# Keys of four chunks loaded instead of transposed, and weights queued in whole pieces, in a retention, mixture and MLP kernel

## The chip, the cores and the metric

The kernel runs on one core of one Trainium2 chip. The metric is the device time of one execution in microseconds (us); lower is better. The kernel before takes 447.51 us (median of 3 runs, 447.18 to 447.83). Beside the runs one execution was profiled, and all rows below come from it.

## The reference

Three parts follow each other. First a linear attention with decay ("retention"), over 4 batches, 8 heads, 768 tokens and 64 features per head; then a soft mixture of 8 experts with 4 slots each; then a two-layer MLP with a sigmoid gate. All is computed in single precision.

```python
def _attn_ref(q, k, v):                       # q, k, v: [4, 8, 768, 64]
    gamma = 1.0 - 2.0 ** (-5.0 - np.arange(H))
    for t in range(S):
        state = gamma * state + einsum('bhd,bhe->bhde', k[:, :, t], v[:, :, t])
        y[:, :, t] = scale * einsum('bhd,bhde->bhe', q[:, :, t], state)

def _moe_ref(x, phi, w1, w2):                 # x: [3072, 512], w1: [8, 512, 1024], w2: [8, 1024, 512]
    logits = x @ phi
    d = softmax(logits over tokens);  slot_input = d.T @ x
    for e in range(8): slot_out[e] = maximum(slot_input[e] @ w1[e], 0) @ w2[e]
    c = softmax(logits over slots);   return c @ slot_out

def _moe2_ref(x, w_in, w_out):                # w_in: [512, 2048], w_out: [2048, 512]
    h = x @ w_in
    return (h / (1 + exp(-1.702 * h))) @ w_out
```

## The kernel before, in words

The kernel has three stages in time. The **retention stage** goes through 24 chunks of 128 tokens (4 batches of 6). The **expert stage** runs the 8 experts on 32 slot inputs; its weights `w1` and `w2` come in 32 pieces of 1 MB. The **MLP stage** takes the rest of the time, on TensorE.

*A chunk.* For chunk i `stage_a` forms the score products of keys and queries (line 211, sixteen matmuls), and VectorE masks them (L215). `stage_v` scales the values on GpSimd (L229). One step later `stage_b` computes the output from the running state (L256) and from the scores (L260), and then adds this chunk's keys times values to the state (L268), except in the last chunk of a batch. `stage_c` transposes the output (L281). Every fourth chunk adds logits (L313) and an outer product (L371).

*Keys, twice.* The score products want the keys with features on the partitions, as they are stored in `ktv`. The state update wants them with tokens on the partitions. That second form comes in one of two ways, which the table `KTP` chooses for each chunk. For a chunk in `KTP`, TensorE transposes the keys it already has (L222, four matmuls into a tile `kp`), and ScalarE copies them out (L223). For any other chunk `load_b` loads them from `kt` in memory (L200, 256 KB).

*Loads.* All loads of this stage are issued by SyncE, in the order of the program, and wait there for their buffer. For chunk i + 2 these are `load_a`: keys and values together (`ktv`, L186, 512 KB in rows of 4 KB) and then the queries (`qt`, L188, 256 KB in rows of 2 KB). There are three buffers of each, so a load waits for chunk i - 1 to be done with its buffer: for the queries that is the state product of that chunk (L256).

*Weights among the chunks.* Seventeen of the 32 weight pieces are loaded in this stage, into 14 buffers of a pool `wp` and 3 of a pool `wq`. `load_half` does it in halves: L129 allocates a piece and loads its first half (512 KB, rows of 4 KB), L124 the second. In every step i > 0 the main loop issues halves, ahead of the step's other loads, until a line through 34 halves at i = 23 is reached. Five more pieces go into the space that the retention tiles leave at the end, and the last ten into buffers of `wp` that the first expert matmuls free; these come through `load_piece` (L137), one transfer of 1 MB with rows of 8 KB, but for the last piece.

TensorE runs its instructions in program order. The order within a step is: scores of i, transposed keys of i if i is in `KTP`, output and state of i - 1, transposed output of i - 2.

Of the kernel before, what the change touches and what calls it, by code (L numbers as in the profile page):

```python
# [24 lines left out]
NI = B * NC  # L25
# [8 lines left out]
NW = 14  # L34
NQ = 3
# [3 lines left out]
FULL = (2, 6, 7)  # L39
Q = 256  # L40
NWU = 3
I0 = 1
SKEW = 128
KTP = (0, 1, 2, 3, 8, 13, 16, 20)
BUD = 2.3
C1, C2 = 0.34, 0.6
WL = (3, 2)
# [3 lines left out]
def retention_soft_moe_mlp(  # L51
# [17 lines left out]
    def pool(stack, name, bufs, **kw):  # L69
        e = ctx.enter_context(ExitStack())  # L70
        kw.setdefault("reuse_waits", "tile")
        if "space" not in kw:
            kw["side"] = "left" if stack is left else "right"
        t = e.enter_context(tc.tile_pool(name=name, bufs=bufs, **kw))
        return t, e
# [4 lines left out]
    wp, _ = pool(left, "wp", NW)  # L80
    sm, sm_e = pool(right, "sm", 2)
    xx, xx_e = pool(right, "xx", 5)
    wq, wq_e = pool(left, "wq", NQ)
# [3 lines left out]
    def wt(tag, shape, name):  # L87
        return fresh.pop(tag, None) or wk.tile(shape, F32, tag=tag, name=name)
# [32 lines left out]
    def load_half(pool):  # L121
        if half:
            t, src = half.pop()
            nc.sync.dma_start(out=t[:, 2:4], in_=src[:, 2:4])  # L124
            return
        kind, e, k = pieces.pop()
        t = pool.tile([P, 4, 512], F32, tag="w", name=f"{kind}_{e}_{k}")
        src = (w1 if kind == "w1" else w2)[e, k, :, 0:2048].rearrange("p (j f) -> p j f", j=4)
        nc.sync.dma_start(out=t[:, 0:2], in_=src[:, 0:2])  # L129
        W[kind, e, k] = t  # L130
        half.append((t, src))

    def load_piece(pool, tag="w"):
        kind, e, k = pieces.pop()
        t = pool.tile([P, 4, 512], F32, tag=tag, name=f"{kind}_{e}_{k}")
        src = (w1 if kind == "w1" else w2)[e, k, :, 0:2048].rearrange("p (j f) -> p j f", j=4)
        nc.sync.dma_start(out=t, in_=src)  # L137
        W[kind, e, k] = t
# [36 lines left out]
    def load_a(i):  # L175
        if i < NI:
            src = ktv[i, :, 0:1024].rearrange("p (a t) -> p a t", a=2)
            if i == 2:
                early.append(wp.tile([P, 4, 512], F32, tag="w", name="early"))
                ktv_t[i] = early[0][:, 0:2]  # L180
            else:
                ktv_t[i] = wt(f"ktv{i % 3}", [P, 2, 512], f"ktv{i}")
            if i < 2:
                nc.sync.dma_start(out=ktv_t[i][:, 0], in_=src[:, 0])
            else:
                nc.sync.dma_start(out=ktv_t[i], in_=src)  # L186
            qt_t[i] = wt(f"qt{(i + 1) % 3}", [P, NP, P], f"qt{i}")
            nc.sync.dma_start(out=qt_t[i], in_=qt[i, :, 0:512].rearrange("p (a t) -> p a t", a=NP))  # L188
# [4 lines left out]
    def load_b(i):  # L193
        if i < NI and i % NC < NC - 1:
            if i == 3:
                t = early[0][:, i].rearrange("p (h d) -> p h d", h=H)
            else:
                t = wt(f"kt{(i - i // NC) % 3}", [P, H, D], f"kt{i}")
            if i not in KTP:
                nc.sync.dma_start(out=t, in_=kt[i, :, 0:512].rearrange("p (h d) -> p h d", h=H))  # L200
            kt_t[i] = t
# [3 lines left out]
    def stage_a(i):  # L205
        q_, kv = qt_t[i], ktv_t[i]
        kT = kv[:, 0].rearrange("p (a t) -> p a t", a=NP)
        sc = [ps.tile([P, NP, P], F32, tag=f"sc{hh}", name=f"sc{hh}_{i}") for hh in range(2)]
        for a in range(NP):
            for hh in range(2):  # L210
                mm(sc[hh][:, a, :], lhsT=kT[hh * D:(hh + 1) * D, a, :], rhs=q_[hh * D:(hh + 1) * D, a, :],  # L211
                   start=True, stop=True)
        pt = [wt(f"pt{hh}{i % 2}", [P, NP, P], f"pt{hh}_{i}") for hh in range(2)]
        for hh in range(2):
            nc.vector.tensor_tensor(  # L215
                out=pt[hh], in0=sc[hh], in1=mask[:, None, :].to_broadcast([P, NP, P]), op=ALU.mult
            )
        p_t[i] = pt
        if i in KTP and i % NC < NC - 1:
            kp = ps.tile([P, NP, P], F32, tag="m", name=f"kp{i}", bufs=3)  # L220
            for a in range(NP):
                nc.tensor.transpose(kp[:, a, :], kT[:, a, :], ident)  # L222
            nc.scalar.copy(out=kt_t[i].rearrange("p h d -> p (h d)"), in_=kp.rearrange("p a t -> p (a t)"))  # L223

    def stage_v(i):
        c = i % NC
        v_ = ktv_t.pop(i)[:, 1].rearrange("p (h d) -> p h d", h=H)
        vt = wt(f"vt{i % 2}", [P, H, D], f"vt{i}")
        nc.gpsimd.tensor_tensor(  # L229
            out=vt, in0=v_, in1=vs[:, c, :, None].to_broadcast([P, H, D]), op=ALU.mult  # L230
        )
        vt_t[i] = vt
        if c == 0:
            tb_t[i] = tab
        else:
            tb_t[i] = wt("tb", [P, NP, P], f"tb{i}")
            nc.gpsimd.tensor_tensor(
                out=tb_t[i], in0=tab, in1=gsc[:, :, c, None].to_broadcast([P, NP, P]), op=ALU.mult
            )
# [3 lines left out]
    def stage_b(i):  # L243
        c = i % NC
        q_, vt, pt = qt_t.pop(i), vt_t.pop(i), p_t.pop(i)
        y = ps.tile([P, 2, 512], F32, tag="y", name=f"y{i}")

        def out_(a, hh):
            o = hh ^ (a & 1)
            return y[o * D:(o + 1) * D, a % 2, P * (a // 2):P * (a // 2) + P]  # L250

        if c > 0:
            for a in range(NP):
                for hh in range(2):
                    r = slice(hh * D, (hh + 1) * D)
                    mm(out_(a, hh), lhsT=s_sb[r, a, :], rhs=q_[r, a, :], start=(a < 2), stop=False,  # L256
                       skip_group_check=True)
        for a in range(NP):
            for hh in range(2):
                mm(out_(a, hh ^ (a & 1)), lhsT=vt[:, 2 * a + (hh ^ (a & 1)), :], rhs=pt[hh ^ (a & 1)][:, a, :],  # L260
                   start=(c == 0 and a < 2), stop=True, skip_group_check=True)
        if c < NC - 1:
            if c == 0:
                st_p[0] = ps.tile([P, NP, D], F32, tag="st", name=f"st{i}")
            st, k_ = st_p[0], kt_t.pop(i)
            for a in range(NP):
                for hh in range(2):
                    mm(st[hh * D:(hh + 1) * D, a, :], lhsT=k_[:, 2 * a + hh, :], rhs=vt[:, 2 * a + hh, :],  # L268
                       start=(c == 0 and a == 0), stop=True, skip_group_check=True)
            nc.scalar.copy(out=s_sb, in_=st)  # L270
        xT = xx.tile([P, NP, P], F32, tag="xT", name=f"xT{i}")
        nc.vector.tensor_tensor(
            out=xT.rearrange("p (s k) t -> p k s t", k=2), in0=y[:, :, 0:2 * P].rearrange("p k (s t) -> p k s t", s=2),
            in1=tb_t.pop(i).rearrange("p (s k) t -> p k s t", k=2), op=ALU.mult,
        )
        xT_t[i] = xT
# [578 lines left out]
    with tc.manual_schedule():  # L855
# [18 lines left out]
        loaded = 0  # L874
        ex_t = {}
        for i in range(NI + 2):
            if i == 2:
                stage_b(1)
            if i < NI:
                stage_a(i)  # L880
                stage_v(i)
                while i > 0 and loaded < min(2 * (NW + NQ), 2 + i * 2 * (NW + NQ) // (NI - I0)):
                    load_half(wp if loaded < 2 * NW else wq)
                    loaded += 1
                load_b(i + 1)
                load_a(i + 2)
            if i >= 8 and i % 4 == 0 and i < NI:
                ex_t[i // 4 - 2] = row_softmax(i // 4 - 2)
            if i >= 9 and i % 4 == 1 and i < NI:
                row_norm(i // 4 - 2, ex_t.pop(i // 4 - 2))  # L890
            if 1 <= i <= NI and i != 2:
                stage_b(i - 1)
            if i >= 2:
                n = i - 1
                g = n // 4 - 1
                if i < NI + 1:
                    stage_c(i - 2)
                else:
                    lp = stage_g1(g, True)
                    stage_c(i - 2, True)  # L900
                    softmax_stats(g, lp)
                    combine1()
                    last_z = stage_g2(g)
                    stage_c2(i - 2)
                if n % 4 == 0 and i <= NI:
                    stage_g1(g)
                if n % 4 == 1 and n > 4:
                    stage_g2(g)
                if n % 4 == 2 and 4 < n < 22:
                    stage_g3(g)  # L910
# [340 lines left out]
```

## Time and profile before

| | |
|---|---|
| runs | 447.51 us median (447.18 to 447.83) |
| profiled execution | 446.99 us |
| its span, first to last instruction | 445.2 us |
| TensorE busy | 433.4 us, 97% |
| VectorE busy | 333.6 us, 75% |
| ScalarE busy | 205.2 us, 46% |
| GpSimd busy | 47.9 us, 11% |
| moved by DMA | 92.38 MB, mean 208 GB/s |

The profile names engines PE (TensorE), DVE (VectorE), ACT (ScalarE), POOL (GpSimd) and SP (SyncE). A busy share over the whole span mixes the stages, so the page also cuts the span into 40 slices. "Share" of the DMA engines is the time that their packets took, as a part of the time of 16 engines; packets overlap a little, so it can stand above 1.

### The profile page before, as it was taken

The numbers are of one execution on the slowest core, as the hardware profiler recorded it, in microseconds if no ns is written. First come the engines' busy times: TensorE is split into PE (matmuls) and PEld (weight loads), VectorE is DVE, ScalarE is ACT, GpSimd is POOL, SyncE is SP. The second block draws the span as 40 slices with busy tenths as digits, with TensorE's granted clock in tenths as the row PEclk, the third lists the DMA queues.
The fourth block names the chain that finished last, engine by engine and source line by source line (L and its number), as shares of the span: only waits on it lengthen the run. The fifth ranks groups of instructions, "written<-read, shape, count | busy, mean of one in ns | idle before, by whom it ended". The sixth has DMA issues, their size and how long they took to land.

```text
span 445.2 us, 9917 instructions
## 1 busy us (share of the span) xinstructions
PE 433.4 (97%) x4105; PEld 359.8 (81%) x4105; DVE 333.6 (75%) x600; ACT 205.2 (46%) x351; POOL 47.9 (11%) x53
## 2 busy tenths in 40 slices
PE   8899999999999899999999999999999999999996
PEld 4787877878333377788888799999999999999995
DVE  2445756665566688897979599997797797988984
ACT  1223232333121275565566656655555555565530
POOL 2453443534000000000000000000000000000000
PEclk9999999999999999999999999999999999999999
DMA  8999999999999776885836402001301301411012
GB/s 308 407 402 403 402 398 400 396 402 346 355 421 400 311 265 208 275 291 191 263 128 190 177 2 95 1 1 47 143 1 48 143 1 49 141 49 48 32 65 94
DMA packets 27662, 92.38 MB, mean 208 GB/s; under 512 B 2865, under 2 KB 4289, under 8 KB 23265
## 3 DMA queue, kind: packets, MB, share of 16 engines
q1 hardware_dynamic: 27248, 91.24, 54.9%
q8 instruction: 32, 0.52, 0.5%
q10 hardware_dynamic: 288, 0.36, 0.2%
q0 software_dynamic: 80, 0.15, 0.1%
q14 instruction: 14, 0.11, 0.1%
HBM read 79.16 MB, written 12.58 MB: 206 GB/s over the span
## 4 chain that ended last, share of the span: by engine, by line
PE 87%; DMA 6%; DVE 3%; ACT 1%; issue 1%; POOL 0%; DVEq 0%; SPq 0%; ACTq 0%
PE P L731 35%; PE acc L668 18%; PE sc L211 5%; DMA qt<-qt_dram 4%; PE y L260 4%; PE hb L697 4%; PE hp L489 3%; PE eo L514 3%; PE y L256 2%; PE xp L281 2%; PE P L841 2%; PE st L268 1%; PE op L371 1%; PE h L645 1%; DMA early<-ktv_dram 1%; PE lp L313 1%
## 5 line engine op out<-in xcount | busy, mean ns | idle before, releaser
L692 DVE TENSOR_TENSOR forms<-forms 128x256 f32<-128x256 f32 (+1 forms) x93 | 47.6, 512 | 22.4 <-ACT forms L699 21.0
L699 ACT ACTIVATE forms<-hb 128x512 f32<-128x512 f32 x62 | 37.2, 599 | 54.7 <-PE hb L697 34.9
L668 PE MATMUL acc<-wo_hl,gh 128*128 128x512 f32 x192 | 59.8, 394 | 0.4 <-ACT gh L647 0.4
L731 PE MATMUL P<-bh,la 128*128 128x256 f32 x208 | 59.0, 284 | 0.0
L731 PE MATMUL P<-bl,ha 128*128 128x256 f32 x208 | 58.8, 283 | 0.0
L731 PE MATMUL P<-bh,ha 128*128 128x256 f32 x208 | 58.7, 282 | 0.0
L731 PE MATMUL P<-bh,hs 128*128 128x256 f32 x156 | 44.1, 283 | 0.0
L731 PE MATMUL P<-bh,ls 128*128 128x256 f32 x156 | 44.0, 282 | 0.0
L731 PE MATMUL P<-bl,hs 128*128 128x256 f32 x156 | 44.0, 282 | 0.0
L215 DVE TENSOR_TENSOR pt<-sc,ca_t 128x512 f32<-128x512 f32 x44 | 28.3, 685 | 18.9 <-PE sc L211 18.9
L668 PEld LDWEIGHTS acc<-wo_hl,gh 128*128 128x128 f32 x192 | 35.4, 188 | 8.0 <-issue 0.6
L731 PEld LDWEIGHTS P<-bl,ha 128*128 128x128 f32 x208 | 39.3, 189 | 1.2
L731 PEld LDWEIGHTS P<-bh,ha 128*128 128x128 f32 x208 | 39.4, 189 | 0.0
L731 PEld LDWEIGHTS P<-bh,la 128*128 128x128 f32 x208 | 39.3, 189 | 0.1
L692 DVE TENSOR_TENSOR la<-forms,ha 128x1024 fp32r<-128x1024 f32 x31 | 37.9, 1223 | 0.0
L668 PE MATMUL acc<-wo_hl,gl 128*128 128x512 f32 x96 | 37.4, 394 | 0.4 <-DVE gl L655 0.4
L715 ACT CAST ha<-forms 128x1024 fp32r<-128x1024 f32 x31 | 32.6, 1051 | 6.5 <-DVE forms L692 5.6
L647 ACT ACTIVATE gh<-h 128x512 fp32r<-128x512 f32 x30 | 18.0, 601 | 33.0 <-PE h L645 24.2
L715 ACT CAST hs<-forms 128x768 fp32r<-128x768 f32 x31 | 26.0, 838 | 10.2 <-DVE forms L692 7.5
L731 PEld LDWEIGHTS P<-bl,hs 128*128 128x128 f32 x156 | 29.5, 189 | 1.2
L692 DVE TENSOR_TENSOR ls<-forms,hs 128x768 fp32r<-128x768 f32 x31 | 29.5, 952 | 0.0
L731 PEld LDWEIGHTS P<-bh,hs 128*128 128x128 f32 x156 | 29.5, 189 | 0.0
(224 smaller groups left out, 909.4 us busy)
## 6 DMA issues: line engine op xcount, KB each, us to landing
w<-w_dram SPq DMA_DIRECT2D x36, 512.0 KB, 7.2
w<-w_dram SPq DMA_DIRECT2D x14, 1024.0 KB, 8.5
ktv<-ktv_dram SPq DMA_DIRECT2D x20, 512.0 KB, 8.1
wi<-w_in_dram SPq DMA_DIRECT2D x7, 1024.0 KB, 5.4
wo<-w_out_dram SPq DMA_DIRECT2D x7, 1024.0 KB, 5.8
parts<-stage SPq DMA_DIRECT2D x24, 256.0 KB, 2.9
pt<-parts SPq DMA_DIRECT2D x6, 1024.0 KB, 4.7
qt<-qt_dram SPq DMA_DIRECT2D x21, 256.0 KB, 6.3
```

Source lines behind the costliest of these rows:

```text
L211: mm(sc[hh][:, a, :], lhsT=kT[hh * D:(hh + 1) * D, a, :], rhs=q_[hh * D:(hh + 1) * D, a, :], start=True, stop=True)
L215: nc.vector.tensor_tensor(out=pt[hh], in0=sc[hh], in1=mask[:, None, :].to_broadcast([P, NP, P]), op=ALU.mult)
L260: mm(out_(a, hh ^ (a & 1)), lhsT=vt[:, 2 * a + (hh ^ (a & 1)), :], rhs=pt[hh ^ (a & 1)][:, a, :], start=(c == 0 and a < 2), stop=True, ski ...
L489: mm(hp[32 * j:32 * j + 32, :], lhsT=slotT[:, k, SPE * (j // 2):SPE * (j // 2) + NS], rhs=w[:, j, :], start=(k == 0), stop=(k == KDM - 1))
L514: mm(op[32 * j:32 * j + 32, :], lhsT=hT[:, kk, 32 * j:32 * j + 32], rhs=w[:, j, :], start=(kk == 0), stop=(kk == 3))
L647: nc.scalar.activation(out=gh, in_=hp, func=AF.Gelu_apprx_sigmoid)
L668: mm(acc[t], lhsT=g[:, t * P:(t + 1) * P], rhs=w, start=f == f0 and n == 0, stop=f == f1 and n == 2)
L692: nc.vector.tensor_tensor(out=out_, in0=a, in1=b_, op=op)
L697: mm(PB["h"], lhsT=gst[:, f * P:(f + 1) * P], rhs=cT[:, 512 * b:512 * b + 512], start=True, stop=True)
L699: nc.scalar.activation(out=t[:, 3 * a:3 * a + 2].rearrange("p s d -> p (s d)"), in_=PB["h"], func=AF.Gelu_apprx_sigmoid)
L715: nc.scalar.copy(out=AH[n, k], in_=FT[0][:, c0:c1])
L731: mm(PB[p][:, t], lhsT=g[:, c], rhs=w, start=r == span_[b][0] and t == 0 and i == 0, stop=r == span_[b][1] - 1 and i == 2, skip_group_chec ...
```

## The change

Two constants and one loop differ. `KTP` keeps the first four chunks alone, so the keys of chunks 8, 13, 16 and 20 come by `load_b`. The weights of the stage are issued by `load_piece`, a whole piece at a time, on another line: one piece in step 1, fifteen more up to step 21, and the seventeenth in step 22, in which no chunk is loaded any more. `I0` goes.

```diff
-I0 = 1
 SKEW = 128
-KTP = (0, 1, 2, 3, 8, 13, 16, 20)
+KTP = (0, 1, 2, 3)
...
-                while i > 0 and loaded < min(2 * (NW + NQ), 2 + i * 2 * (NW + NQ) // (NI - I0)):
-                    load_half(wp if loaded < 2 * NW else wq)
+                while 0 < i and loaded < (1 + (i - 1) * (NW + NQ - 2) // (NI - 4) if i < NI - 2 else NW + NQ):
+                    load_piece(wp if loaded < NW else wq)
                     loaded += 1
                 load_b(i + 1)
                 load_a(i + 2)
```

Two places of SyncE's order show it. The first is around chunk 8, in the kernel before. A name such as `ktv8_495` is the tile of chunk 8 and a running number; `w1_1_1` is piece 1 of the second part of `w1`; 128x1024 is half a weight piece, 128x2048 a whole one.

```order
L188 DMA qt7_413<-qt_dram 128x512
L124 DMA w1_1_0_407<-w1_dram 128x1024
L200 DMA kt7_493<-kt_dram 128x512
L186 DMA ktv8_495<-ktv_dram 128x1024
L188 DMA qt8_497<-qt_dram 128x512
L129 DMA w1_1_1_547<-w1_dram 128x1024
L124 DMA w1_1_1_547<-w1_dram 128x1024
L186 DMA ktv9_551<-ktv_dram 128x1024
L188 DMA qt9_553<-qt_dram 128x512
```

The same place in the changed kernel, where the lines are smaller by one:

```order
L187 DMA qt7_407<-qt_dram 128x512
L199 DMA kt7_486<-kt_dram 128x512
L185 DMA ktv8_488<-ktv_dram 128x1024
L187 DMA qt8_490<-qt_dram 128x512
L136 DMA w1_1_0_540<-w1_dram 128x2048
L199 DMA kt8_542<-kt_dram 128x512
L185 DMA ktv9_544<-ktv_dram 128x1024
L187 DMA qt9_546<-qt_dram 128x512
```

A load of `kt8` has come in between, in front of chunk 9's loads, and the weights come whole, at this place a piece later than before.

The second place is the end of the stage, in the kernel before:

```order
L186 DMA ktv22_1498<-ktv_dram 128x1024
L188 DMA qt22_1500<-qt_dram 128x512
L124 DMA w1_2_3_1494<-w1_dram 128x1024
L129 DMA w2_1_0_1564<-w2_dram 128x1024
L200 DMA kt22_1566<-kt_dram 128x512
L186 DMA ktv23_1568<-ktv_dram 128x1024
L188 DMA qt23_1570<-qt_dram 128x512
L124 DMA w2_1_0_1564<-w2_dram 128x1024
L137 DMA w2_1_1_1855<-w2_dram 128x2048
```

And in the changed kernel:

```order
L185 DMA ktv22_1461<-ktv_dram 128x1024
L187 DMA qt22_1463<-qt_dram 128x512
L136 DMA w1_2_3_1526<-w1_dram 128x2048
L199 DMA kt22_1528<-kt_dram 128x512
L185 DMA ktv23_1530<-ktv_dram 128x1024
L187 DMA qt23_1532<-qt_dram 128x512
L136 DMA w2_1_0_1624<-w2_dram 128x2048
L136 DMA w2_1_1_1818<-w2_dram 128x2048
```

Ahead of the queries of the last chunk, `qt23`, stand 33 halves before and 16 whole pieces now; the piece `w2_1_0` is whole behind them, where only its second half stood.

## Rows read from the trace of the kernel before

**Rows 1.** Page, the span in 40 slices of 11.1 us, tenths busy.
```profile
PE   8899999999999899999999999999999999999996
...
DMA  8999999999999776885836402001301301411012
```

**Rows 2.** Chain of waits in order of time: start us, us, what.
```profile
10.92 6.83 DMA qt<-qt_dram
...
20.29 5.84 DMA qt<-qt_dram
...
39.96 0.59 PE kp L222 x4
...
45.08 6.91 DMA qt<-qt_dram
...
92.23 0.58 PE kp L222 x4
...
104.28 1.16 PE sc L211 x16
```

**Rows 3.** Waits of TensorE up to 117 us: us in total, times, longest.
```profile
PE sc L211 <- DMA qt<-qt_dram: 0.9, 2, 0.7
```

**Rows 4.** SyncE's issues for chunk 23: start us, us, engine, line, tiles.
```profile
95.48 0.38 SPq L186 DMA_DIRECT2D ktv<-ktv_dram  x1
97.35 0.33 SPq L188 DMA_DIRECT2D qt<-qt_dram  x1
97.73 0.43 SPq L124 DMA_DIRECT2D w<-w_dram  x1
```

**Rows 5.** Queries of chunk 23: issue (ns, start us), then us to landing.
```profile
L188 SPq DMA_DIRECT2D qt<-qt_dram x1: 328/328/328, 97.3 to 97.3; - x1
...
DMA to landing us min/median/max: 6.8/6.8/6.8
```

**Rows 6.** Queries of chunk 2: the same.
```profile
L188 SPq DMA_DIRECT2D qt_first<-qt_dram x1: 566/566/566, 4.1 to 4.1; - x1
...
DMA to landing us min/median/max: 7.9/7.9/7.9
```

**Rows 7.** Stretches: us, busy us and instructions by engine, clock, DMA share, GB/s.
```profile
12.00:104.20 92.20, 90.31 (x1573) 73.69 (x1569) 55.13 (x110) 27.96 (x73) 39.84 (x40) 1.00 1.03 401
104.20:117.00 12.80, 11.92 (x170) 8.04 (x169) 6.67 (x18) 3.63 (x11) 3.12 (x5) 1.00 0.92 325
126.00:137.00 11.00, 11.00 (x100) 3.50 (x96) 8.93 (x38) 2.27 (x4) 0.00 (x0) 1.00 1.01 422
```

**Rows 8.** ScalarE's copies of transposed keys: ns min/median/max, first and last start.
```profile
L223 ACT COPY kt<-kp x4: 586/586/587, 40.6 to 92.9; 128x512 f32<-128x512 f32 x4
```

**Rows 9.** DMA packets from 126 to 137 us.
```profile
DMA packets 631, 4.65 MB, mean 422 GB/s; under 512 B 64, under 2 KB 64, under 8 KB 64
```

**Rows 10.** DMA packets and queues from 12 to 104.2 us, share of 16 engines.
```profile
DMA packets 12455, 36.97 MB, mean 401 GB/s; under 512 B 1388, under 2 KB 1388, under 8 KB 12412
...
q1 hardware_dynamic: 12438, 36.72, 101.9%
q8 instruction: 13, 0.21, 0.9%
q14 instruction: 4, 0.03, 0.1%
```

**Rows 11.** Query loads from 10 to 98 us, us to landing.
```profile
DMA to landing us min/median/max: 4.7/6.3/8.3
```

**Rows 12.** One whole weight piece behind the stage: issue, us to landing.
```profile
L137 SPq DMA_DIRECT2D w<-w_dram x1: 328/328/328, 106.1 to 106.1; - x1
...
DMA to landing us min/median/max: 5.5/5.5/5.5
```

**Rows 13.** Waits of SyncE from 96 to 118 us: us in total, times, longest.
```profile
SPq L137 <- PE sc L211: 6.8, 2, 3.4
SPq L137 <- PE op L371: 4.6, 1, 4.6
```

## The prediction

> **What bounds the kernel now.** I read four views, from the whole to the one place that decides.
>
> First the slices of the page [rows 1]. The PE row stands at 8 to 9 tenths nearly throughout. The DMA row stands at 8 and 9 only in the first thirteen slices (11.1 us each). So there are two stretches: up to some 145 us the loads and TensorE are both full, and afterwards TensorE alone. The change touches the retention stage, which ends near 116 us.
>
> Second, the chain of waits in order of time [rows 2]. It is nearly all TensorE, but three times it runs through the load of a chunk's queries: from 10.92, 20.29 and 45.08 us. The last score products (chunk 23) start at 104.28 us. TensorE's own waits [rows 3] put only 0.9 us down to these loads, so by that view alone TensorE would be the bound.
>
> Third, the load queue's order [rows 4]. SyncE issues the queries of chunk 23 at 97.35 us; they need 6.8 us to land [rows 5], so they land at 104.2, and the products that read them start at 104.28. There is no room left at that place: the queue delivers the last chunk just as TensorE is ready for it. The queries of chunk 2, issued at 4.1, landed after 7.9 us [rows 6], at 12.0. Between these two landings lie 92.2 us, in which the DMA engines are busy at a share of 1.03 with 401 GB/s [rows 7]. So the queue never pauses, and chunk 23 can't come sooner than the sum of what is queued ahead of it. That sum is what I work out.
>
> **The change, part by part.** *What leaves TensorE.* Chunks 8, 13, 16 and 20 lose four transposes each. In the chain such a group is 0.59 us, the first at 39.96, the last (0.58) at 92.23 [rows 2]; four of them are 2.36 us, all on the path. ScalarE loses four copies of 0.586 us [rows 8]; it is busy 28.0 of 92.2 us there [rows 7], so that is worth nothing.
>
> *What the queue gets ahead of chunk 23.* Counted in SyncE's order: four more key loads of 256 KB; sixteen whole pieces of 1 MB in place of 33 halves of 512 KB, so half a piece less; the seventeenth piece follows behind the queries of chunk 23. The bytes alone are 4 x 0.262 - 0.524 = +0.52 MB, at 401 GB/s 1.3 us more.
>
> *What whole pieces save.* A half is 128 rows of 4 KB, a whole piece 128 rows of 8 KB. From 126 to 137 us the queue carries whole pieces alone: 631 packets, 64 of them tiny (each transfer ends with 16), the other 567 over 8 KB [rows 9]. Over 16 engines and 11.0 us that is 0.310 us for one packet of 8,192 bytes. From 12.0 to 104.2 us the main queue has 12,438 packets, 1,388 of them tiny, so 11,050 data packets, with 36.72 MB; the instruction queues take 1.0% [rows 10]. So 16 engines carried them in 91.3 us. Two equations, with a price per packet p and per byte b: 8,192 b + p = 310 ns, and 36.72 MB x b + 11,050 p = 16 x 91.3 us. They give p = 10.5 ns and b = 36.6 ns per 1,000 bytes. An engine takes 8 rows of every transfer, so: keys of a chunk 8 x 85.5 ns = 0.68 us, a half 8 x 160.5 ns = 1.28, a whole piece 8 x 310 ns = 2.48, which is 0.08 less than two halves.
>
> The sum for the landing of chunk 23's queries: 4 x 0.68 = +2.74; one half less, -1.28; 16 x 0.084 = -1.34; together +0.12 us. The 2.36 us that TensorE saves don't reach the end; they become waiting for loads, in pieces of some tenths at several chunks.
>
> The saving is the unknown term, because no whole piece stands in the mixed queue before. Its ends: with p = 0 (no saving, b from the whole pieces) the sum is 4 x 0.62 - 1.24 = +1.24 us. With the plain rates, 401 GB/s for all of the stage and 422 for whole pieces [rows 7], a piece saves 2.61 - 2.48 = 0.13, so 4 x 0.65 - 1.31 - 16 x 0.13 = -0.8 us. I take the middle one, +0.1, which rests on both stretches.
>
> The Trainium skill, "DMA: Bandwidth & Descriptors", section "Why small descriptors are slow (HBM only)", speaks against a saving here: beside a few cycles per packet a descriptor costs a fixed 32 bytes on the fabric, and joining consecutive ones pays only at 256 bytes or less. By that rule 4 KB and 8 KB rows would cost the same per byte, which is the first rival below. The trace disagrees so far: 10.5 ns per packet is what 290 bytes take.
>
> *Chunks on the way.* A whole piece makes the queue lumpier: a chunk behind one waits 2.48 instead of 1.28 us, one without a piece gets its loads early. TensorE now has 2.36 us of spare time to make it up and the end goes by the sum, so this costs nothing unless the queue runs dry. The shortest time from issue to landing of queries was 4.7 us [rows 11]; a lone transfer in the quiet time behind the stage (1 MB, issued at 106.1) took 5.5 us [rows 12], of which 2.5 are its own, so some 3 us are latency. Of the 4.7 the queries' own 0.7 and these 3 leave about 1 us that the thinnest queue had in hand. I put 0.3 us for a dry moment into the upper end.
>
> The keys that are now loaded stand ahead of the next chunk's values and queries in the queue, and that chunk's score products come before the state update that reads the keys. So no new wait forms on them.
>
> *Behind the last chunk.* The seventeenth piece lands there whole, 1.2 us more than the half that stood there (97.73 in [rows 4]). The next loads can't use that time anyway: SyncE holds them until TensorE frees the buffers, 6.8 us for score products and 4.6 us for the last outer products [rows 13], and the share of the DMA engines falls to 0.92 from 104.2 to 117 [rows 7]. If that cover were gone it would cost 1.2 us. From 104.28 on TensorE's work is the same as before, so what happens to chunk 23 is passed on to the end.
>
> *Sum.* The profiled execution took 446.99 us (span 445.2 and 1.8 around it). With +0.1 it is 447.1. It ran 0.5 us under the median of 447.51, so the median becomes 447.6.
>
> **Rivals.**
> 1. *Slower: whole pieces cost the same per byte.* Place: the sixteen pieces ahead of chunk 23. The price is +1.24 us, so 448.75. It decides when a whole piece takes 2.55 us or more in the mixed queue. For it: the 10.5 ns come from two stretches with different company. Against it: 422 against 401 GB/s.
> 2. *Faster: TensorE is the bound, and the loads have room.* Then the 2.36 us come through: 445.2. For it: TensorE is at 9 tenths and its recorded waits on loads are 0.9 us. Against it: the landing at 104.2 against 104.28, and the three loads in the chain.
> 3. *Faster by the queue: whole pieces run better than 2.48 us.* At the plain rates the end comes 0.8 us sooner, 446.7; with 2.40 us a piece (437 GB/s) it is 16 x 0.08 = 1.3 us below the forecast, 446.3.
>
> **Chances.** About 0.2% (0.9 us) is what a measurement of this kernel can tell from no change. The queue sets the end and the sum is near nothing: 0.57, with a range of its own from 446.7 to 448.4. Rival 1: 0.17. Rival 2: 0.11. Rival 3 down to its lower end: 0.15. Faster takes rival 2 and most of rival 3, 0.25. Slower takes rival 1 and a little of the forecast's upper end, 0.21. The rest, 0.54, is within 0.2%. The range is 446.0 to 449.0; it leaves out rival 2 and a dry queue on top of rival 1.
>
> **What would show it.** In the changed profile: no transposes of chunks 8, 13, 16 and 20; score products that wait for query loads at several chunks, some 2 us in all, where 0.9 stood; the queries of chunk 23 landing at about 104.3, and their products within 0.2 us of that; from there to the end the same time as before. A landing near 105.5 is rival 1; products of chunk 23 well behind their landing, near 102, are rival 2; a landing under 103.5 is rival 3. I am wrong altogether if the stage keeps its time and the expert stage moves.

## The result, and the profile after

The changed kernel takes 450.07 us (median of 6 runs, 449.19 to 452.15), the kernel before 447.48 (6 runs beside it). The ratio is 1.0058, 95% interval 1.0034 to 1.0082: slower by 0.6%. I had forecast 447.6 and no change, with a range up to 449.0; the time lies outside it. (Ratios here and below leave out executions in which the chip ran in a slower state; medians and spreads are over all.) The profiled execution of the changed kernel took 451.68 us, with a span of 449.9. That is 1.6 us above the median, so what its trace shows is larger than the usual loss.

The slices of the page, as [rows 1], and with them the granted clock and the rate:

```profile
PE   8997998999999989999999999999999999999996
...
PEclk9998999999999999999999999999999999999999
DMA  8999999999999958687655502001311301311012
GB/s 312 366 375 399 344 386 407 405 400 406 350 414 412 399 196 282 189 290 272 189 186 188 185 2 96 1 0 48 101 42 47 133 9 47 142 48 46 26 71 93
```

The DMA row looks like the one before. The rate does not: counted from 0, slices 1, 2, 4 and 5 have 366, 375, 344 and 386 GB/s. TensorE has gaps (7 tenths in slice 3, 8 in slice 6), and its granted clock shows 8 tenths in slice 3. The rate in the slices of the kernel before:

```profile
GB/s 308 407 402 403 402 398 400 396 402 346 355 421 400 311 265 208 275 291 191 263 128 190 177 2 95 1 1 47 143 1 48 143 1 49 141 49 48 32 65 94
```

The chain of waits, start us, us, what; it answers to [rows 2]:

```profile
27.28 9.19 DMA qt<-qt_dram
36.47 0.14 issue
36.61 1.97 PE sc L210 x16
38.58 1.82 PE y L259 x16
...
64.04 9.15 DMA qt<-qt_dram
...
83.92 7.12 DMA qt<-qt_dram
...
101.19 7.64 DMA qt<-qt_dram
108.82 0.14 issue
108.96 1.16 PE sc L210 x16
...
110.72 1.02 PE y L259 x16
```

The chain runs through query loads as foretold, and the last one sets the end of the stage: the queries of chunk 23 land at 108.82, and their products start 0.14 us later. But that is 4.6 us after the landing before ([rows 4, 5]: 97.35 + 6.8), not 0.1. From those products to the end nothing moved: 449.9 - 108.96 = 340.9 us, and before 445.2 - 104.28 = 340.9.

TensorE's own waits on these loads went from 0.9 us [rows 3] to 5.7, where the prediction had some 2:

```profile
PE sc L210 <- DMA qt<-qt_dram: 5.7, 4, 2.9
```

Where the queue lost the time, by stretches of the changed kernel (columns as in [rows 7]; the last two are the share of the DMA engines and GB/s):

```profile
12.00:32.00 20.00, 19.53 (x356) 16.49 (x353) 9.47 (x16) 5.89 (x14) 9.24 (x9) 1.00 0.99 366
32.00:37.00 5.00, 2.11 (x25) 1.73 (x27) 1.41 (x3) 0.75 (x2) 1.01 (x2) 0.98 1.04 407
37.00:42.00 5.00, 5.00 (x60) 4.07 (x56) 1.98 (x3) 0.37 (x1) 2.03 (x3) 0.68 1.04 415
42.00:47.00 5.00, 5.00 (x85) 3.98 (x81) 3.16 (x6) 1.77 (x4) 0.75 (x2) 1.00 0.90 324
47.00:52.00 5.00, 5.00 (x108) 4.27 (x108) 3.38 (x10) 1.10 (x4) 2.86 (x4) 1.00 1.00 401
52.00:57.00 5.00, 5.00 (x95) 4.18 (x95) 3.33 (x7) 1.86 (x7) 2.59 (x3) 1.00 0.88 327
...
12.00:104.20 92.20, 86.25 (x1484) 70.34 (x1479) 51.86 (x103) 24.40 (x63) 37.68 (x37) 0.98 1.00 386
```

Two of these stretches in the kernel before:

```profile
12.00:32.00 20.00, 18.64 (x344) 15.94 (x340) 9.06 (x15) 5.52 (x12) 9.82 (x10) 1.00 1.03 405
...
42.00:47.00 5.00, 5.00 (x94) 4.26 (x90) 3.13 (x8) 1.48 (x4) 2.05 (x2) 1.00 1.03 403
```

Read it as a sequence. From 12 to 32 us TensorE has not waited for a single query load yet (the first of its four waits is chunk 7's), and still the queue moves 366 GB/s, not 405. That is 0.78 MB less, some 1.9 us at 401 GB/s. In steps 1 to 3 the new line issues two pieces, 2 MB, and the old line six halves, 3 MB. So the first loss is a lack of queued work. From 32 to 37 us the queue is full, at 407 GB/s, and TensorE works 2.11 of 5 us: it waits for the queries of chunk 7, which stand behind the third of three whole pieces in three successive steps and take 9.19 us to land. From 42 to 47 it is the other way: TensorE is busy, and the queue falls to a share of 0.90 and 324 GB/s. In between stands SyncE (start us, us, engine, line, tiles):

```profile
35.85 0.33 SPq L187 DMA_DIRECT2D qt<-qt_dram  x1
36.49 0.33 SPq L136 DMA_DIRECT2D w<-w_dram  x1
40.90 0.33 SPq L199 DMA_DIRECT2D kt<-kt_dram  x1
41.33 0.77 SPq L185 DMA_DIRECT2D ktv<-ktv_dram  x1
44.45 0.33 SPq L187 DMA_DIRECT2D qt<-qt_dram  x1
```

Between 36.8 and 40.9 it issues nothing. The key load at 40.90 waits 3.7 us for a buffer that state products free (L267), and these come behind the late products of chunk 7. SyncE's waits from 12 to 104 us, us in total, times, longest:

```profile
SPq L199 <- PE st L267: 9.5, 7, 3.7
```

The next queries go out at 44.45, and by then little is queued. So from here on the loads and TensorE hold each other up in turn. The spread from issue to landing of the queries is wider at both ends, against 4.7 / 6.3 / 8.3 before [rows 11]:

```profile
DMA to landing us min/median/max: 3.9/6.0/9.2
```

### The profile page after: what moved, and what is told of

Its sections match the earlier page's. It is cut to its first block, busy times and chain, and to the rows that moved or that the text cites. A ratio compares the mean times of both kernels' runs of the same rounds, so it can differ in the third digit from the quotient of the medians.

```text
span 449.9 us, 9871 instructions
## 1 busy us (share of the span) xinstructions
PE 433.3 (96%) x4089; PEld 360.0 (80%) x4089; DVE 333.6 (74%) x600; ACT 202.7 (45%) x347; POOL 47.8 (11%) x53
## 4 chain that ended last, share of the span: by engine, by line
PE 86%; DMA 7%; DVE 3%; ACT 1%; issue 1%; SPq 0%; DVEq 0%; ACTq 0%
PE P L730 35%; PE acc L667 18%; DMA qt<-qt_dram 7%; PE sc L210 5%; PE y L259 4%; PE hb L696 4%; PE hp L488 3%; PE eo L513 3%; PE y L255 2%; PE P L840 2%; PE xp L280 2%; PE st L267 1%; PE op L370 1%; PE h L644 1%; PE wu L870 1%
## 5 line engine op out<-in xcount | busy, mean ns | idle before, releaser
L210 PEld LDWEIGHTS sc<-qt,ktv 64*128 64x128 f32 x320 | 20.6, 193 | 12.9 <-issue 9.8
L210 PE MATMUL sc<-qt,ktv 64*128 64x128 f32 x320 | 24.5, 291 | 6.4 <-DMA qt<-qt_dram 5.7
```

## The experiments

Eleven kernels ran, 6 to 12 executions each, beside the kernel before (medians 447.24 to 447.31; its single executions reach 451.27). The stage has two choices in them: how the four chunks' keys come, and how the weights are cut and spread. After this trace I had three theories: D, the new line queues too little in the first ten steps and the queue runs dry; W, whole pieces with rows of 8 KB are themselves served unevenly; B, only the 0.5 MB more.

**x1, halves on the new line.** The changed kernel, with two halves for each piece, in the same place.

```diff
-                    load_piece(wp if loaded < NW else wq)
+                    load_half(wp if loaded < NW else wq)
+                    load_half(wp if loaded < NW else wq)
```

> The changed kernel, but each weight piece of the retention stage goes as two halves of 512 KB right behind each other, in the same place of the order. Theory D (the load queue runs dry in the first ten steps, because on the new line one to two halves less are queued ahead of each chunk): the dry stretches stay, and the halves' extra packets add up to 1.2 us: 449.5 to 451.3, with shares of the DMA engines under 1.0 between 20 and 60 us as in the changed kernel. Theory W (whole pieces themselves are served unevenly, 3.0 to 4.2 us where 2.5 are nominal): the excess goes, only the sum of the queue (+1.2) is left: 448.3 to 448.9, share 1.03 throughout. Theory B (only the 0.5 MB more ahead of chunk 23): 448.8.

451.23 us (449.92 to 453.04), ratio 1.0071 (1.0038 to 1.0105). The time that D expected came. W falls: without any row of 8 KB it is as slow. By the medians it is 1.2 us slower than the changed kernel, near the 1.34 us that my sum has for the packets, but the two intervals overlap. B, which gives 448.8, falls too.

**x2, the keys alone.** The kernel before with the short table.

```diff
-KTP = (0, 1, 2, 3, 8, 13, 16, 20)
+KTP = (0, 1, 2, 3)
```

> The kernel before, with the keys of chunks 8, 13, 16 and 20 loaded instead of transposed; the weights stay in halves on the old line. All theories: the queue is longer by four loads of 0.66 us, chunk 23's queries land 2.6 to 2.7 us later, near 106.9, and the time is 450.0 to 450.2. Theory D adds that the queue stays at a share of 1.03 throughout, so that the runs scatter by no more than those of the kernel before. If TensorE had been the bound, the time would fall by up to 2.4 us to 445.1.

450.16 us (449.58 to 455.56), ratio 1.0070 (1.0046 to 1.0095). The scatter is not as small as expected: one execution stands at 455.56, the other eleven at 450.96 or less. The queue is the bound: +2.9 us where the sum had +2.74, and none of TensorE's 2.36 us comes through. Its queue is full to the end, at the same rate as before (from 12 to 104.2 us):

```profile
12.00:104.20 92.20, 86.43 (x1510) 70.31 (x1510) 53.16 (x106) 24.83 (x66) 38.90 (x38) 1.00 1.03 401
```

**x3, the line alone.** The changed kernel with the long table of before.

```diff
-KTP = (0, 1, 2, 3)
+KTP = (0, 1, 2, 3, 8, 13, 16, 20)
```

> The kernel before with the weights whole and on the new line, and the keys of the eight chunks transposed as before. By the plain sum of the queue the last chunk would come 2.5 us sooner, and TensorE, which keeps its transposes, would then limit the gain to 1 to 1.5 us: 446.0 to 446.5. Theory D: the queue is as thin as in the changed kernel or thinner (four loads less), it runs dry in the first ten steps, and most of the gain is lost: 447.0 to 449.5. Theory W: the same loss, since the whole pieces are the same.

448.39 us (447.07 to 454.56), ratio 1.0014 (0.9992 to 1.0035): not to be told from no change, where the sum of the queue gives 446.0 to 446.5. Some 2 us are missing by that sum; against x11 below, which has the same keys and pieces in even halves, it is 1.5 us by the medians. So the loss belongs to the weights, not to the keys.

**x4, whole pieces on the old line.** The changed kernel, each piece in the step in which its second half was issued before.

```diff
-                while 0 < i and loaded < (1 + (i - 1) * (NW + NQ - 2) // (NI - 4) if i < NI - 2 else NW + NQ):
+                while 0 < i and loaded < min(NW + NQ, (2 + i * 2 * (NW + NQ) // (NI - 1)) // 2):
```

> The changed kernel, but the whole pieces go on the old line (a piece is issued in the step in which its second half was issued before), which puts up to one piece more ahead of the chunks in steps 2 to 20; step 22 has the seventeenth as in the changed kernel. Theory D: the queue hardly runs dry any more, and the sum that I had worked out holds, +0.1: 447.3 to 448.3, shares of 1.02 or 1.03 in the first ten steps. Theory W: the pieces are as uneven as in the changed kernel: 449.5 to 450.5.

450.37 us (448.47 to 451.15), ratio 1.0055 (1.0031 to 1.0079). This spoke against D, my own theory: the old line doesn't help. It is the time that W expected, but x1 had ruled W out. x1, x3 and x4 have one thing in common, and x2 lacks it: the weights go out 1 MB a step for two or three steps in a row, and then a step has none. The 1 MB alone is not it, since x2 too has eleven steps up to 21 with two halves or more; but none of its steps goes empty. That is theory L, the lump.

The granted clock is not needed for the loss. x1 and x4 lost their time in profiled executions that kept it at 1.00 (x1 first; they took 450.26 and 451.00 us):

```profile
12.00:104.20 92.20, 86.48 (x1516) 70.32 (x1511) 53.85 (x107) 25.19 (x67) 38.99 (x38) 1.00 1.02 393
...
12.00:104.20 92.20, 84.47 (x1476) 68.74 (x1474) 52.10 (x103) 24.39 (x63) 37.72 (x38) 1.00 1.01 392
```

**x5, rows of 8 KB without the lump.** x2, but a half is now every other row of a piece: 64 rows of 8 KB instead of 128 rows of 4 KB.

```diff
-        nc.sync.dma_start(out=t[:, 0:2], in_=src[:, 0:2])
+        nc.sync.dma_start(out=t[0:P:2], in_=src[0:P:2])
...
-            nc.sync.dma_start(out=t[:, 2:4], in_=src[:, 2:4])
+            nc.sync.dma_start(out=t[1:P:2], in_=src[1:P:2])
```

> The kernel with the four chunks' keys loaded and the weights on the old line in single halves (which took 450.2), but a half is now every other row of a piece, so 64 rows of 8 KB: the same packets as a whole piece's, without its lump of 1 MB in one step. Theory L (lumps: whole pieces, or two halves at once, leave steps without a weight, in which the queue runs dry, and delay the queries behind them, so that the next loads are issued late): only the saving on packets shows, 33 x 0.04 = 1.4 us, so 448.5 to 449.1, little scatter, no stretch under a share of 1.0. Theory W (packets of 8 KB are themselves served unevenly in the mixed queue): 450.0 to 452.

448.82 us (448.48 to 449.55), ratio 1.0031 (1.0021 to 1.0041). Against x2 the larger packets save 1.34 us, where 33 halves at 0.042 give 1.39. W, which gives 450.0 to 452, is out for good, and the packet term of my sum holds.

**x6, the lump alone.** The kernel before, its halves of 4 KB rows issued two at a time.

```diff
-                while i > 0 and loaded < min(2 * (NW + NQ), 2 + i * 2 * (NW + NQ) // (NI - I0)):
-                    load_half(wp if loaded < 2 * NW else wq)
+                while i > 0 and loaded < min(NW + NQ, (2 + i * 2 * (NW + NQ) // (NI - I0)) // 2):
+                    load_half(wp if loaded < NW else wq)
+                    load_half(wp if loaded < NW else wq)
                     loaded += 1
```

> The kernel before with one difference: its halves of 512 KB (rows of 4 KB) are issued two at a time, in the step in which the second one was issued before; keys transposed as before. By the sum of the queue half a piece less stands ahead of chunk 23, so nothing is lost: 446.5 to 447.3 for theory W, since no packet is larger. Theory L: the lumps alone make it slower than the kernel before, 448.0 to 449.5, with more scatter.

448.90 us (447.31 to 452.35), ratio 1.0036 (1.0018 to 1.0054). Nothing but the grouping is changed, half a piece less stands ahead of chunk 23, and the kernel is slower. The last queries don't set its end: they land at 105.0 (issue 99.17, 5.8 us), and their products start at 106.06, behind TensorE's own work. With all its transposes TensorE has no time to win its waits back. The query loads take from 3.6 to 9.5 us:

```profile
DMA to landing us min/median/max: 3.6/5.8/9.5
```

And the rate of the stage falls to 393 GB/s, against 401 in [rows 7]:

```profile
12.00:104.20 92.20, 88.88 (x1542) 72.36 (x1538) 53.68 (x108) 27.56 (x71) 39.26 (x39) 1.00 1.02 393
```

**x7, rows of 8 KB on the kernel before.** The edit of x5 with the long table.

> The kernel before, keys transposed and the old line as they were; a half is every other row of a piece (64 rows of 8 KB). Theory L and the packet price: the queue gets 1.4 us shorter, and TensorE, which was ready at 104.28 for a landing at 104.19, takes part of it through its earlier waits: 446.3 to 447.1. Theory W: 448 or more.

446.47 us (445.98 to 448.50), ratio 0.9986 (0.9972 to 1.0000). As expected of L. TensorE waits 0.7 us for queries, and the products of chunk 23 follow its own work without a wait; it is nearly the bound again.

**x8, the changed kernel without the lump.** Keys of the four chunks loaded, sixteen pieces ahead of chunk 23 and one behind it, rows of 8 KB, but as single halves (x5's), one or two in each step.

```diff
-                while i > 0 and loaded < min(2 * (NW + NQ), 2 + i * 2 * (NW + NQ) // (NI - I0)):
+                while i > 0 and loaded < (2 + i * (2 * (NW + NQ) - 4) // (NI - 3) if i < NI - 2 else 2 * (NW + NQ)):
```

> The changed kernel without its lumps: keys of the four chunks loaded, sixteen pieces ahead of chunk 23 and the seventeenth behind it, packets of 8 KB, but as single halves of 64 rows spread evenly, one or two a step. The queue holds the very sum that my prediction worked out for the changed kernel. Theory L: the sum then holds, 447.3 to 448.2, against 450.1 for the changed kernel. Theory W: 449.5 or more. If it comes out like the changed kernel, neither lumps nor the sum explain it.

447.79 us (447.61 to 448.15), ratio 1.0008 (0.9998 to 1.0018). It puts the same bytes in packets of the same size ahead of chunk 23 as the changed kernel, and it is 2.3 us faster by the medians (ratios 1.0008 and 1.0058), at the place where my sum had put the changed kernel (447.6). Its runs scatter by 0.5 us, those of the changed kernel by 3. No step of it goes without weights; ten steps up to 21 have two halves or more. Its query loads from issue to landing:

```profile
DMA to landing us min/median/max: 5.4/6.6/7.7
```

The longest takes 7.7 us instead of 9.2. Its stretch from 12 to 104.2 us, with the rate in the last column:

```profile
12.00:104.20 92.20, 87.80 (x1537) 71.69 (x1538) 53.86 (x109) 25.14 (x67) 38.99 (x38) 1.00 1.03 406
```

**x10, whole pieces, never behind.** What about the lump costs: that a piece comes late (D, once more), or its size in front of a query load? Here each whole piece is issued as soon as the even line has begun it.

```diff
-                while 0 < i and loaded < (1 + (i - 1) * (NW + NQ - 2) // (NI - 4) if i < NI - 2 else NW + NQ):
+                while 0 < i and loaded < ((3 + i * (2 * (NW + NQ) - 4) // (NI - 3)) // 2 if i < NI - 2 else NW + NQ):
```

> The changed kernel with whole pieces, but each issued in the step in which the even line has begun it, so that the queue never holds less than on the even line (447.8); sixteen pieces ahead of chunk 23 as there. What about a lump costs? Theory D, the lack: a whole piece comes too late on the new line and the queue runs dry; then this kernel, which is never behind, comes out like the even line, 447.6 to 448.5, with little scatter. Theory L, the lump itself: a query load behind 2.5 us of weights lands late, TensorE waits and frees the next buffer late, and a step without weights then finds the queue short, whatever stands ahead at the start: 449.3 to 450.5, with scatter.

451.04 us (450.57 to 455.75), ratio 1.0117 (1.0076 to 1.0158): the slowest of all by the ratio, 0.5 us beyond what L expected, though at no step is less queued than on the even line. Its chain of waits, start us, us, what:

```profile
9.49 9.34 DMA qt<-qt_dram
18.82 0.14 issue
18.96 1.29 PE sc L210 x16
20.25 1.04 PE kp L221 x4
21.30 1.06 PE y L255 x16
...
107.95 0.11 PE ep L358
108.06 1.09 PE sc L210 x16
```

And SyncE's issues there:

```profile
5.44 0.84 SPq L136 DMA_DIRECT2D w<-w_dram  x2
...
9.49 0.58 SPq L187 DMA_DIRECT2D qt<-qt_dram  x1
...
13.54 0.33 SPq L187 DMA_DIRECT2D qt<-qt_dram  x1
13.91 0.44 SPq L136 DMA_DIRECT2D w<-w_dram  x1
15.05 0.33 SPq L199 DMA_DIRECT2D kt<-kt_dram  x1
15.42 0.43 SPq L185 DMA_DIRECT2D ktv_first<-ktv_dram  x1
22.42 0.33 SPq L187 DMA_DIRECT2D qt<-qt_dram  x1
```

Two pieces stand ahead of chunk 3's queries, where the even line has three halves, and the queries land after 9.34 us. TensorE starts chunk 3 at 18.96 (17.89 before, 16.58 in x8) and runs it slowly, so the next query load waits for its buffer until 22.42 (20.29 before, [rows 2]). Between 22 and 27 us the rate is 338 GB/s:

```profile
22.00:27.00 5.00, 5.00 (x84) 4.18 (x78) 1.68 (x3) 0.96 (x2) 2.05 (x2) 0.87 0.92 338
```

So a queue that was too full a moment before is too empty now. D as I had put it, too little ahead, is refuted as the whole cause: x4 and x10 have more ahead and are as slow. The changed kernel's first loss, from 12 to 32 us, is such a lack all the same: it moves 368 GB/s from 12 to 22 us, where x4 and x10, with three pieces in steps 1 to 3, move 402 and 410. Here in x10 the dry moment follows from a late query instead.

Most of the loss of this execution falls at that one place. Chunk 3 starts 2.4 us later than in x8, chunk 23 2.9 us later. In x8 chunk 23's products start at

```profile
105.17 1.16 PE sc L223 x16
```

and wait there for their queries. In x10 they stand behind TensorE's own work (108.06 in the chain above), and the last queries had landed at 107.0. In x4, too, they landed 1.0 us before their products began. So in these two the late queries of chunks on the way cost TensorE time that it didn't win back.

**x9, a better version.** x8, with chunks 13 and 20 transposed again.

```diff
-KTP = (0, 1, 2, 3)
+KTP = (0, 1, 2, 3, 13, 20)
```

> The even line with half pieces of 64 rows, and only chunks 8 and 16 loaded, 13 and 20 transposed. Theory of the sum: the queue is 2 x 0.66 = 1.3 us shorter than with all four loaded (447.8), so 446.5 if the queue is still the bound; TensorE has two groups of transposes (1.2 us) less than the kernel before, so it allows about 446. Both theories of the lump say the same, since none is left: 446.0 to 446.7, faster than both kernels of the change.

446.18 us (445.94 to 447.73), ratio 0.9979 (0.9970 to 0.9989): faster than both kernels of the change. TensorE waits 1.1 us for queries, against 4.3 in x8, and the last queries land (103.2) just before their products start (103.31), so loads and TensorE are about in balance:

```profile
PE sc L223 <- DMA qt<-qt_dram: 1.1, 2, 0.7
```

**x11, the even line with all eight chunks transposed.** x8 with the long table.

> The even line with half pieces of 64 rows, and all eight chunks transposed as before: against the kernel that had rows of 8 KB on the old line (446.5) one half less stands ahead of chunk 23. If TensorE is the bound there, nothing is gained: 446.2 to 446.8. If the queue still was, 1.3 us are gained: 445.2.

446.90 us (445.93 to 447.45), ratio 0.9987 (0.9978 to 0.9995). It has the least queued ahead of chunk 23 and isn't faster than x9 or x7. I had expected 446.2 to 446.8 if TensorE is the bound, and the time is 0.1 us above that. But the trace doesn't show TensorE alone as the bound. In its profiled execution (447.02 us) the only wait for queries is at chunk 23 itself:

```profile
PE sc L223 <- DMA qt<-qt_dram: 0.8, 1, 0.8
...
96.65 7.59 DMA qt<-qt_dram
...
104.37 1.16 PE sc L223 x16
```

The last load still ends last there, though the queue holds less than in x7. Why it comes so late stays open; a rate of 369 and 356 GB/s from 72 to 82 us shows that the queue was not full all the time.

Not tried: a fourth buffer for the queries, which would let a load be issued earlier. Whether lumps would then be harmless stays open.

## Why the prediction was wrong

*The bound was right.* In the changed kernel the last queries set the end of the stage, to 0.14 us, and what TensorE saves doesn't come through (x2). Rival 2 is out. After chunk 23 nothing changed, as I had written.

*The terms of the sum were right.* Four key loads: +2.74 foretold, +2.9 measured (x2). Packets: -1.34 foretold for sixteen pieces; x5 against x2 has -1.34 for 33 halves where -1.39 follows from the same price, and the changed kernel against x1 has -1.2. The half piece moved behind: -1.28 foretold, x8 against x5 has -1.03 by the medians. Together x8 stands 0.5 us above the kernel before by the medians, 0.08% by the ratio, where the sum says +0.12. So rival 1, no saving (+1.24), is out as well, and so is rival 3 (-0.8). The Trainium skill ("DMA: Bandwidth & Descriptors", section "Why small descriptors are slow (HBM only)") says that joining consecutive descriptors pays only up to 256 bytes. Read as a rule on rows of 4 KB, as the prediction read it, this is not borne out by x5 here, and the measurement decides.

*The step that failed* is the one on the chunks on the way: "the end goes by the sum, so this costs nothing unless the queue runs dry", with 0.3 us for a dry moment. The lumps cost 2.3 us: 450.07 against 447.79 for the same bytes in packets of the same size without lumps (x8), and 4.6 us at chunk 23 in the profiled execution of 451.68 us. I treated the queue as work that is all there, and TensorE as a reader with time to spare. But SyncE issues a query load only when TensorE has freed the buffer of three chunks before. So a query has some 7 us from issue to use (97.35 to 104.28 for chunk 23 of the kernel before, where a chunk takes 4.3 us), and in [rows 11] the loads already took 4.7 to 8.3 us. With the weights in lumps the queue is at times too short, as from 12 to 32 us of the changed kernel. At other times it is so long that a query lands late; TensorE waits, frees its buffers late, and the next loads are issued late. In the changed kernel this is time of the queue, which is the bound: 386 GB/s from 12 to 104.2 us where x8 has 406. The spare 2.36 us of TensorE can't make that up.

That lumps are enough by themselves x6 shows; that too little ahead is not the whole cause x4 and x10 show. A size of 1 MB ahead of a query is not enough: ten or eleven steps of the even kernels have that too. What all the slow kernels share, and no even one has, is two or three steps in a row with 1 MB each and then a step with none (five or six such steps up to 21). Whether the full steps or the empty ones cost more no run separates. Nor is it separated how much of the changed kernel's 2.3 us is the clock (below); x1, x4 and x6 lose time with the clock at 1.00 throughout the stage.

## What to carry to other kernels

Where loads wait for buffers that the consumer frees, a full queue isn't a fixed sum. Look at both ends of the spread from issue to landing of the load that the consumer needs, not only at the total: in x1 the longest (8.5 us) is no longer than in x2 (8.6), but the shortest is 3.4 instead of 5.3. Spread background loads evenly, so that no step goes without. If larger rows are wanted, cut the transfer by rows and not by columns: the packets stay large and the lump stays small. An edit that takes work from an engine that waits for the queue, and gives the queue more, gains nothing on the one side and pays on the other (x2).

## What was not expected of the hardware

After TensorE's wait of 2.9 us for chunk 7 the granted clock was 0.98 in the stretch 32 to 37 and 0.68 in the next five us, so for part of it the lower of its two levels (1.2 and not 2.4 GHz); the sixteen score products took 1.97 us instead of 1.16, and the sixteen products behind them 1.82 instead of 1.02. That made this late load dearer by 1.6 us on TensorE. In x10 it came after chunk 3's wait of 1.9 us, with 0.79 from 17 to 22 us and 0.87 from 22 to 27. In x8, whose longest wait was 1.2 us, and in x4, whose longest was 1.8, the clock stood at 1.00.

Half a piece as 64 rows of 8 KB, every other partition, runs at least as fast as 128 rows of 4 KB: 406 GB/s in the mixed queue of x8, against 401 before.
